# A fused GELU MLP, forward and backward: single steps up to pair 11 with x units as fill, and b2 added by VectorE

## The chip, the cores and the metric

The kernel runs on one core of a Trainium2 chip. The metric is the device time of one execution in microseconds (us). Engines: TensorE (PE, its weight loads PEld), VectorE (DVE), ScalarE (ACT), GpSimd (POOL) and SyncE (SP, which issues most transfers).

## The reference

An MLP with tanh-GELU, and all its gradients by `jax.vjp`; everything is bfloat16:

```python
B, S, D, F = 1, 2048, 448, 1792
h = gelu(x @ w1 + b1, approximate=True)      # (S, F)
out = h @ w2 + b2                            # (S, D)
# returns out and, for grad_out: grad x, grad w1, grad b1, grad w2, grad b2
```

So per block of rows the kernel needs u = x w1 + b1, h = gelu(u), out = h w2 + b2, q = grad_out w2^T, gh = q * gelu'(u), grad x = gh w1^T; at the end grad w1 = x^T gh and grad w2 = h^T grad_out, and the sums for the biases.

## The kernel before

**Tiling.** The 2048 rows are four blocks of 512 (0 to 3). F = 1792 is 14 tiles of 128, taken two at a time: a "pair" of tiles, seven per block, 28 in all. They are numbered k = 0 to 27 through the blocks; pair k belongs to block k // 7. For each one TensorE makes u (two banks of PSUM, [128, 512] each, list `PU`) and q (one double bank, `PQ`). D = 448 is three full tiles of 128 and a rest of 64 (`KF` = 3, `DL` = 64); the rest is the "tail" (`u_tail`, `q_tail`), a product over 64 rows of the array.

**Half products.** `half_product` (line 263) is a product over 64 of the 128 rows of the array, and `side_by_side` sends two of them, one on the lower and one on the upper half of the rows, into two different banks. A full product (lines 242, 303, 430) uses all 128 rows. Where halves and full products change places, a product of one kind follows one of the other.

**Units.** A "unit" is 128 rows of an output: kind "o" for out (from hT and w2), kind "x" for grad x (from ghT and w1T), with 14 tiles to be summed in one bank. Block by block there are four o units and four x units; `todo` holds them in that order, `open_unit` takes the next one and gives it a bank. They fill TensorE's time between the u and q products. `units_side` makes two units at once by halves: once with `second` False and once with True, so that each unit gets both halves of each tile. `pieces` and `Unit.emit` make them with full products. A unit that is finished waits in `finished` until `evictions` writes it out: by ScalarE (line 441) for x units and for the o units of block 0, whose b2 TensorE adds by a product with `row0`, a tile that has ones in two rows (`b2_of`); by VectorE with b2 added (line 443) for the other o units.

**The chain of a pair.** ScalarE or VectorE copies u out of its banks and adds b1 (`copy_u`, lines 346 and 348); ScalarE makes the square of u (line 355), gelu(u) into hT (352) and later a tanh (364). VectorE makes from the square the argument of the tanh ("cubic", "cubic*u"), from the tanh and h the slope of gelu ("slope", "slope*h", "both", "gate"), and at last `dve_gh` (line 400), gh = slope * q, which reads q's banks and frees them.

**Single steps and pairs.** The order on each engine is the order in which the code issues (`manual_schedule`); nothing reorders it. After the start (pairs 0, 1 and the u of 2) there are single steps i = 1 to 7 (`NSINGLE` = 8): a step makes u for f = i + 2 and q for i, with unit tiles between them (`between`). All these steps use banks 0 and 1 for u, and the double bank `two0` for q. From k = 8 on two pairs are taken at once (a loop over n, ks = [k, k + 1], fs = [k + 2, k + 3]), with instructions of double width; q's banks are then `two0` for even k and `two1` for odd k. In the first two of these rounds u, q and the units are full products (`pe_u_fulls`, `pe_q_fulls`, `pieces(28, ...)`); in the third only u is; after that everything is in halves, the u products of the round after next (`nxt`) are made ahead, and each round opens two units in `two1` as soon as gh has freed it.

In a single step ScalarE's order is tanh i, `evictions(2)`, copy f, `evictions()`, square f, gelu f. VectorE's order in the last single step, i = 7, is:

```python
dve_chain("both 7", "cubic*u 8", "gate 7", "cubic 9", "gh 7", "cubic*u 9")
```

The first two x units of block 0 are opened in `two1` at the end of step 6 and finished at the end of step 7; their eviction is issued at the head of the first pair round. In that round `dve_gate` and `act_tanh` stand at the head, so tanh of the two pairs needs "cubic*u" of both.

**Other lines.** `AZ` holds the squares and tanh arguments of three pairs in turn; `SETS`, `part_a` and `part_z` say where. `traffic` issues the transpositions of gh, the loads of the next block and, in step 6, `other_halves`; `stores` writes h to DRAM for the last phase. `g_low` is a copy of a tail of grad_out on the other half of the rows. After the blocks come grad w1 (line 742) and grad w2 (line 774) as full products.

Of the kernel before, what the change touches and what calls it, by code (L numbers as in the profile page):

```python
# [11 lines left out]
BF16 = mybir.dt.bfloat16  # L12
# [7 lines left out]
def kernel(  # L20
# [15 lines left out]
    nc = tc.nc  # L36
    P = 128
# [11 lines left out]
    NSTEP = NB * NPAIR  # L49
    NSINGLE = 8  # L50
    LEAD = 2
# [91 lines left out]
    nc.gpsimd.memset(b1_rows[:], 0.0)  # L143
    nc.vector.memset(row0[:], 0.0)
    for r0 in (0, DL):
        nc.vector.memset(row0[r0:r0 + 1, :], 1.0)
    nc.gpsimd.dma_start(out=b1_rows[0:NF, :], in_=b1.rearrange("(ft p) -> ft p", p=P))
# [48 lines left out]
    U4 = tmp.tile([P, 4, SB], BF16, name="U4", tag="U4", bufs=1)  # L196
    SETS = [8, 4]

# [121 lines left out]

    def unit_of(un, first, tiles):
        src, w = (hT, w2_sb) if un.kind == "o" else (ghT, w1T_sb)
        return lambda hf: [(un, un.ps, src[un.b][hf, t, un.j * P:(un.j + 1) * P], w[hf, 2 * FP[t // 2] + t % 2, :], hf,
                            first and t == 0, not first and t == NF - 1 and not un.b2_pe) for t in tiles]

    def b2_of(un):
        return lambda hf: [(un, un.ps, row0[hf, :], b2_bc[hf, :], hf, False, hf.start == (0 if un.j % 2 else DL))]

    def units_side(uns, second, tiles=range(NF)):
        one, other = uns[::-1] if second else uns  # L330
        side_by_side(unit_of(one, not second, tiles), unit_of(other, not second, tiles))
        if second and tiles[-1] == NF - 1:
            if one.b2_pe:
                side_by_side(b2_of(one), b2_of(other))
# [82 lines left out]
    class Unit:  # L417
        def __init__(self, kind, b, j):
            self.kind, self.b, self.j, self.done, self.ps = kind, b, j, 0, None
            self.b2_pe = kind == "o" and b == 0  # L420
            self.by_act = kind == "x" or self.b2_pe

# [4 lines left out]
        def emit(self, p):  # L427
            src, w = (hT, w2_sb) if self.kind == "o" else (ghT, w1T_sb)
            for a in range(2):
                nc.tensor.matmul(self.ps, lhsT=src[self.b][:, 2 * p + a, self.j * P:(self.j + 1) * P],  # L430
                                 rhs=w[:, 2 * FP[p] + a, :], start=(p == 0 and a == 0),
                                 stop=(p == NPAIR - 1 and a == 1 and not self.b2_pe), skip_group_check=True)
            if p == NPAIR - 1 and self.b2_pe:
                nc.tensor.matmul(self.ps, lhsT=row0[:], rhs=b2_bc[:], start=False, stop=True, skip_group_check=True)
            self.done += 1

        def evict(self):
            st = stg.tile([P, SB], BF16, name="st", tag="st")
            r = ROW0[self.b] + self.j * P
            if self.by_act:  # L440
                nc.scalar.copy(out=st[:, 0:D], in_=self.ps)  # L441
# [74 lines left out]
    uns = [open_units[0:2], open_units[2:4]]  # L516
    pieces(4, 0, -1)

# [3 lines left out]
    pe_tails([2], [0])  # L522
    side_by_side(q_of(0, 0), q_of(0, 1))
    units_side(uns[0], False, tiles(1))
    side_by_side(q_of(0, 1, True), q_of(0, 0, True))
    dve_chain("slope 0", "slope*h 0", "both 0", "cubic 1", "gate 0", "cubic*u 1", "slope 1", "gh 0", "slope*h 1")
    copy_u(2, "aa")
    act_tanh([1])
    act_square([2])
    act_gelu([2])  # L530
    for i in range(1, NSINGLE):
# [10 lines left out]
        units_side(*between[0])  # L542
        side_by_side(u_of(f, 1), u_of(f, 0))
        units_side(*between[1])
        pe_tail_pair(f, i, 1)
        pe_tail_pair(f, i, 0)
        units_side(*between[2])
        side_by_side(q_of(i, 0), q_of(i, 1))
        units_side(*between[3])
        side_by_side(q_of(i, 1, True), q_of(i, 0, True))  # L550
        if i < 6:
            units_side(uns[0], False, tiles(i + 1))
        if i > 1:
            act_tanh([i])
        evictions(2)
        copy_u(f, "aa")
        evictions()
        act_square([f])
        act_gelu([f])
        if i == 1:  # L560
            dve_chain("both 1", "cubic 2", "gate 1", "cubic*u 2", "slope 2", "gh 1", "slope*h 2", "cubic 3")
        elif i < 7:
            dve_chain(f"both {i}", f"cubic*u {i + 1}", f"gate {i}", f"slope {i + 1}", f"gh {i}", f"slope*h {i + 1}", f"cubic {f}")
        else:
            dve_chain("both 7", "cubic*u 8", "gate 7", "cubic 9", "gh 7", "cubic*u 9")
        if i == 6:
            open_two(1, 2)
            uns = [open_units[-2:]]
            units_side(uns[0], False, range(0, 6))
# [6 lines left out]
    g_swap = {}  # L576
    g_low = const.tile([P, SB], BF16, name="g_low")
    nq = NSTEP // 2 - NSINGLE // 2

    def two_units(banks):  # L580
        for n in banks:
            open_unit(one_bank(n, "ps")[:, 0:D])
        return open_units[-2:]

# [10 lines left out]
    for n in range(nq):  # L595
        i = NSINGLE + n
        k = NSINGLE + 2 * n
        ks = [k, k + 1]
        fs = [k + 2, k + 3] if k + 2 < NSTEP else []
        nxt = [k + 4, k + 5] if n >= 2 and k + 4 < NSTEP else []  # L600
        if n == 0:
            evictions()
        act_tanh(ks)
        dve_gate(ks, evictions)
        if n <= 2:
            for f in fs:
                pe_u_fulls(f)
        if n < 2:
            pe_tails(fs, ks)
            for q in ks:  # L610
                pe_q_fulls(q)
            for f in fs:
                copy_u(f, "aa")
            for q in ks:
                dve_gh(q)
            open_one()
            pieces(28, k + 1, k - 1)
            act_square(fs)
            act_gelu(fs)
            evictions(1)  # L620
            dve_cubic(fs)
        else:
            if fs:
                pe_tails(fs[::-1], ks[::-1])
            for f in fs[::-1]:
                copy_u(f, "aa")
            pe_q_rows(ks, nxt)
            for q in ks[::-1]:
                dve_gh(q)
            if nxt:  # L630
                open_u(nxt[0])
                side_by_side(u_of(nxt[0], 0, True), u_of(nxt[0], 1, True), slice(0, 1))
                open_two(1, 2)
                uns = open_units[-2:]
                units_side(uns, False)
                side_by_side(u_of(nxt[0], 0, True), u_of(nxt[0], 1, True), slice(1, None))
                units_side(uns, True)
                side_by_side(u_of(nxt[1], 1), u_of(nxt[1], 0))
                side_by_side(u_of(nxt[0], 1), u_of(nxt[0], 0))
            elif fs:  # L640
                uns, held = two_units(order_a[2:4]), two_units(order_a[0:2])
                units_side(uns, False)
                units_side(held, False)
                pe_tails([], [k + 2, k + 3])
                units_side(uns, True)
            if fs:
                act_square(fs)
                act_gelu(fs)
                dve_cubic(fs)
        if i == 8:  # L650
            nc.gpsimd.dma_start(out=g_low[0:DL, :], in_=gT[1][DL:P, 0, :])
            g_swap[1] = g_low
        if i == 15:
# [168 lines left out]
```

## Time and profile before

| | us |
|---|---|
| median of 3 runs | 269.21 (268.45 to 270.72) |
| profiled execution | 268.56 |
| its span | 266.8 |
| TensorE busy | 261.6 (98%) |
| VectorE busy | 173.4 (65%) |
| ScalarE busy | 138.7 (52%) |
| GpSimd busy | 40.3 (15%) |

The span runs from the first to the last instruction; the profiled execution's own time is longer by what lies around it. In lines of the timeline the columns are start, duration, engine, line of the code, operation, output and inputs, shapes, how many were merged, and in brackets the idle time ahead of it and what ended it. Ends of matmuls are modelled; the distance from one start to the next tells what one costs. In lines of waits: who waited for whom, us in total, times, longest.

### The profile page before, as it was taken

How to read it: one execution, taken by the hardware profiler on the slowest of the kernel's cores; microseconds unless marked ns; L12 is line 12 of the kernel's file. 1: busy time of each engine (PE TensorE's matmuls, PEld its weight loads, DVE VectorE, ACT ScalarE, POOL GpSimd, SP SyncE). 2: the span in 40 equal slices, each digit the busy share in tenths (PEclk: the TensorE clock that was granted, in tenths of full speed). 3: DMA queues.
4: the chain of work that ended last, by engine and by line, in shares of the span. 5: the costliest groups of instructions: out<-in, count | busy, mean ns of one | idle time of the engine just before them, and what ended most of it. 6: DMA issues, size and time to landing. Idle time of an engine off the chain costs nothing.

```text
span 266.8 us, 5001 instructions
## 1 busy us (share of the span) xinstructions
PE 261.6 (98%) x2082; PEld 159.9 (60%) x2082; DVE 173.4 (65%) x202; ACT 138.7 (52%) x162; POOL 40.3 (15%) x52
## 2 busy tenths in 40 slices
PE   7999999999999999999999999999999999999995
PEld 3367888744446565555658888864444765555554
DVE  2699997799998979669897731129999990000000
ACT  2899998899986686878659410022111111121111
POOL 1001004101002021010301020220700008900000
PEclk9999999999999999999999999999999999999999
DMA  7999999999999966264361359999511102999961
GB/s 160 252 227 211 175 213 188 288 232 206 259 225 257 220 172 170 54 164 94 111 157 43 72 120 256 357 197 230 138 39 39 52 20 58 200 225 225 161 163 34
DMA packets 111734, 44.46 MB, mean 167 GB/s; under 512 B 91040, under 2 KB 110576, under 8 KB 111712
## 3 DMA queue, kind: packets, MB, share of 16 engines
q1 hardware_dynamic: 104608, 36.14, 65.2%
q10 hardware_dynamic: 5248, 3.71, 5.6%
q0 software_dynamic: 1856, 4.30, 5.3%
q8 instruction: 16, 0.26, 0.4%
q14 instruction: 6, 0.05, 0.1%
HBM read 7.23 MB, written 14.23 MB: 80 GB/s over the span
## 4 chain that ended last, share of the span: by engine, by line
PE 94%; ACT 2%; DMA 2%; DVE 0%; issue 0%; ACTq 0%
PE ps L263 29%; PE ps_v L774 16%; PE ps_w L742 14%; PE pq L263 13%; PE pu L263 12%; PE pu L242 4%; PE ps_w L753 2%; PE pq L303 2%; PE ps L430 2%; DMA xT<-in_x_dram 2%; ACT AZ L355 1%; ACT hT L352 1%; DVE U L348 0%; ACT U L346 0%; ACT AZ L364 0%
## 5 line engine op out<-in xcount | busy, mean ns | idle before, releaser
L263 PE MATMUL ps<-w_sb,hT 64*128 64x448 bf16 x432 | 50.7, 349 | 0.3 <-ACT hT L352 0.3
L263 PE MATMUL pq<-gT,w2T 64*128 64x512 bf16 x338 | 49.9, 376 | 0.0
L774 PE MATMUL ps_v<-g_nat,h_nat 128*128 128x448 bf16 (+1 forms) x240 | 42.6, 340 | 0.0
L400 DVE SCALAR_TENSOR_TENSOR ghT<-AZ,pq 128x1024 bf16<-128x1024 bf16 x28 | 33.9, 1220 | 12.8 <-PE pq L263 11.8
L346 ACT ACTIVATE U<-pu,b1T 128x512 bf16<-128x512 f32 x54 | 33.3, 686 | 17.0 <-PE pu L263 12.7
L263 PE MATMUL ps<-w1T_sb,ghT 64*128 64x448 bf16 x392 | 40.8, 349 | 0.0
L444 POOL DMA_DIRECT2D out_dram<-st x32 | 18.9, 595 | 137.2 <-ACT st L441 84.0
L263 PEld LDWEIGHTS <-hT 64*128 64x128 bf16 x432 | 29.3, 94 | 13.7 <-ACT hT L352 0.8
L742 PE MATMUL ps_w<-gh_nat,x_nat 128*128 128x512 bf16 (+1 forms) x192 | 36.5, 352 | 0.0
L774 PEld LDWEIGHTS <-h_nat 128*128 128x128 bf16 x240 | 23.3, 98 | 19.3 <-DMA out_dram<-st 0.3
L263 PEld LDWEIGHTS <-ghT 64*128 64x128 bf16 x392 | 28.7, 94 | 9.2
L263 PE MATMUL pu<-xT,w_f 64*128 64x512 bf16 x228 | 33.1, 376 | 0.0
L263 PEld LDWEIGHTS <-w2T 64*128 64x128 bf16 x344 | 26.3, 94 | 9.5 <-PE pq L263 0.4
L364 ACT ACTIVATE AZ<-AZ 128x2048 bf16<-128x2048 bf16 (+1 forms) x18 | 27.5, 1526 | 7.4 <-DVE AZ L360 7.3
L728 DVE TENSOR_TENSOR acc<-acc,gh_nat 128x1792 f32<-128x1792 f32 x14 | 30.0, 2142 | 0.5
L742 PEld LDWEIGHTS <-x_nat 128*128 128x128 bf16 x192 | 18.7, 98 | 17.9 <-issue 0.4
L355 ACT ACTIVATE AZ<-U 128x1024 bf16<-128x1024 bf16 (+1 forms) x19 | 27.7, 1460 | 0.8 <-DVE U L348 0.4
L352 ACT ACTIVATE hT<-U 128x1024 bf16<-128x1024 bf16 (+1 forms) x20 | 27.6, 1383 | 0.0
L441 ACT CAST st<-ps 128x448 bf16<-128x448 f32 x20 | 9.8, 531 | 30.9 <-PE ps L263 28.7
L777 ACT CAST st<-ps_v 128x448 bf16<-128x448 f32 (+1 forms) x15 | 7.6, 507 | 34.8 <-PE ps_v L774 34.8
L745 ACT CAST st<-ps_w 128x512 bf16<-128x512 f32 (+1 forms) x12 | 6.4, 532 | 27.2 <-PE ps_w L742 27.2
L263 PEld LDWEIGHTS <-w_f 64*128 64x128 bf16 x228 | 15.6, 94 | 7.9 <-issue 0.2
(60 smaller groups left out, 214.2 us busy)
## 6 DMA issues: line engine op xcount, KB each, us to landing
hT_dram<-hT SPq DMA_DIRECT2D x28, 256.0 KB, 3.0
out_dram<-st POOLq DMA_DIRECT2D x32, 112.0 KB, 3.6
x_nat<-in_x_dram SPq DMA_DIRECT2D x1, 1792.0 KB, 10.7
g_nat<-in_grad_out_dram SPq DMA_DIRECT2D x1, 1792.0 KB, 16.3
out_dram<-st ACTq DMA_DIRECT2D x13, 112.0 KB, 3.6
out_dram<-st ACTq DMA_DIRECT2D x9, 128.0 KB, 1.9
w_f<-in_w_dram SPq DMA_DIRECT2D x5, 192.0 KB, 4.4
w_sb<-in_w_dram SPq DMA_DIRECT2D x4, 224.0 KB, 3.7
```

Source lines behind the costliest of these rows:

```text
L242: nc.tensor.matmul(PU[f][a][:, rs], lhsT=w1_f[:, kt, cols(p, a)], rhs=xT[b][:, kt, rs], start=(kt == 0 and rs.start == 0), stop=False, ski ...
L263: mm = nc.tensor.matmul(ps, lhsT=w, rhs=m, start=start, stop=stop, tile_position=(hf.start, 0), skip_group_check=True)
L346: nc.scalar.activation(out=dst, in_=PU[f][a][:], func=ACT.Identity, bias=bias)
L352: nc.scalar.activation(out=rows(hT, r), in_=part_u(r), func=ACT.Gelu_apprx_tanh)
L355: nc.scalar.activation(out=part_a(ks), in_=part_u(ks), func=ACT.Square, scale=math.sqrt(3.0 * GELU_A * GELU_C))
L364: nc.scalar.activation(out=z, in_=z, func=ACT.Tanh, scale=-1.0 / 3.0)
L400: nc.vector.scalar_tensor_tensor(out=rows(ghT, [k]), in0=part_z([k]), scalar=1.0, in1=PQ[k][:], op0=ALU.subtract if single else ALU.add, o ...
L441: nc.scalar.copy(out=st[:, 0:D], in_=self.ps)
L444: nc.gpsimd.dma_start(out=(out2 if self.kind == "o" else gx2)[r:r + P, :], in_=st[:, 0:D])
L728: nc.vector.tensor_tensor(out=v, in0=in0, in1=gh_nat[:, b, :, j, :], op=ALU.add)
L742: nc.tensor.matmul(ps[:, 0:n * P], lhsT=x_nat[:, st_, kt * P:(kt + 1) * P], rhs=gh_nat[:, b, ft0:ft0 + n, j, :], start=(st_ == 0), stop=(s ...
L774: nc.tensor.matmul(ps[:, 0:w], lhsT=h_nat[ft][:, st_, :], rhs=g_nat[:, st_, h * w:(h + 1) * w], start=(st_ == 0), stop=(st_ == NS - 1))
```

## The change

There are twelve single steps in place of eight (i up to 11), and the loop over pairs begins at k = 12, with all of its products in halves. Steps 7 to 11 each have ten pairs of unit halves as fill, taken from a list of 50: the rest of the first two x units (`ahead`, in `two1`), and the other two x units of block 0 (`later`, in banks 2 and 3). VectorE adds b2 to block 0's o units, as it does for all others; `row0`, `b2_of` and their products go. At the start only the first two units get a piece of full products ahead of the first tails; the first tiles of the other two (units Y and Z, `uns[1]`) come by halves after q's products. VectorE makes half of copy 2, "gate 0" moves behind "cubic*u 1". A unit is now finished by a count of its halves (`slots`).

```diff
-    NSINGLE = 8
+    NSINGLE = 12
-    row0 = const.tile([P, P], BF16, name="row0")
...
-    SETS = [8, 4]
+    SETS = [0, 8]
...
-        return place(4 * (k % 3) + 2 if k < NSINGLE else 2 * (k % 2), ks)
+        return place(4 * (k % 3) + 2 if k < NSINGLE else 4 + 2 * (k % 2), ks)
...
-    def b2_of(un):
-        return lambda hf: [(un, un.ps, row0[hf, :], b2_bc[hf, :], hf, False, hf.start == (0 if un.j % 2 else DL))]
...
-            if self.by_act:
+            if self.kind == "x":
                 nc.scalar.copy(out=st[:, 0:D], in_=self.ps)
...
     uns = [open_units[0:2], open_units[2:4]]
-    pieces(4, 0, -1)
+    for un in uns[0]:
+        un.emit(0)
...
     pe_tails([2], [0])
     side_by_side(q_of(0, 0), q_of(0, 1))
+    units_side(uns[1], False, tiles(0))
+    side_by_side(q_of(0, 1, True), q_of(0, 0, True))
+    units_side(uns[1], True, tiles(0))
     units_side(uns[0], False, tiles(1))
-    side_by_side(q_of(0, 1, True), q_of(0, 0, True))
-    dve_chain("slope 0", "slope*h 0", "both 0", "cubic 1", "gate 0", "cubic*u 1", "slope 1", "gh 0", "slope*h 1")
-    copy_u(2, "aa")
+    dve_chain("slope 0", "slope*h 0", "both 0", "cubic 1")
+    copy_u(2, "av")
+    dve_chain("cubic*u 1", "gate 0", "slope 1", "gh 0", "slope*h 1")
...
-            between = [(uns[0], False, range(6, 10)), (uns[0], False, range(10, 12)), (uns[0], False, range(12, 14)), (uns[0], True, range(0, 6))]
+            if i == 7:
+                ahead, later = xs, two_units((2, 3))
+                slots = [(ahead, False, t) for t in range(6, NF)] + [(later, False, t) for t in range(NF)]
+                slots += [(ahead, True, t) for t in range(NPAIR)] + [(later, True, t) for t in range(NF)]
+                slots += [(ahead, True, t) for t in range(NPAIR, NF)]
+            between = [slots[2 * c:2 * c + 2] for c in range(5)]
+            del slots[0:10]
...
         side_by_side(q_of(i, 1, True), q_of(i, 0, True))
         if i < 6:
             units_side(uns[0], False, tiles(i + 1))
+        elif i > 6:
+            fill(between[4])
         if i > 1:
             act_tanh([i])
-        evictions(2)
+        if i == 6:
+            evictions(2)
         copy_u(f, "aa")
-        evictions()
+        if i > 6:
+            evictions()
         act_square([f])
         act_gelu([f])
...
-            dve_chain("both 7", "cubic*u 8", "gate 7", "cubic 9", "gh 7", "cubic*u 9")
+            dve_chain(f"both {i}", f"cubic*u {i + 1}", f"gate {i}", f"cubic {f}", f"gh {i}", f"cubic*u {f}")
         if i == 6:
+            evictions()
             open_two(1, 2)
...
-        if i == 7:
-            units_side(uns[0], True, range(6, NF))
-        traffic(i)
+        if i == 9:
+            nc.gpsimd.dma_start(out=g_low[0:DL, :], in_=gT[1][DL:P, 0, :])
+            g_swap[1] = g_low
+        if i < 8 or i % 2:
+            traffic(i if i < 8 else (i + 7) // 2)
         if i >= 6:
-            stores(2, f - 1)
+            stores(1 if i > 7 and i % 2 else 2, f - 1)
...
+    def pe_u_rows(fs):
+        for f in fs:
+            open_u(f)
+            side_by_side(u_of(f, 0, True), u_of(f, 1, True))
+        for f in fs:
+            side_by_side(u_of(f, 1), u_of(f, 0))
...
     for n in range(nq):
-        i = NSINGLE + n
+        i = 10 + n
...
-        if n <= 2:
-            for f in fs:
-                pe_u_fulls(f)
-        if n < 2:
-            pe_tails(fs, ks)
...
+        if n == 0:
+            pe_u_rows(fs)
+        if fs:
+            pe_tails(fs if n == 0 else fs[::-1], ks[::-1])
```

In the new kernel's first pair round TensorE's order is: u of 14 and 15 (12 pairs of halves), their tails with those of q 13 and q 12, q 13, q 12, q 13, u 17, q 12, the first products of u 16, then two units in `two1`.

More of the change, by code (lines that the diff above doesn't have):

```diff
@@ L319, in q_of, with unit_of @@
                            for kt in range(1, KF + 1)]
-    def unit_of(un, first, tiles):
+    def unit_of(un, tiles):
         src, w = (hT, w2_sb) if un.kind == "o" else (ghT, w1T_sb)
         return lambda hf: [(un, un.ps, src[un.b][hf, t, un.j * P:(un.j + 1) * P], w[hf, 2 * FP[t // 2] + t % 2, :], hf,
-                            first and t == 0, not first and t == NF - 1 and not un.b2_pe) for t in tiles]
-    def b2_of(un):
-        return lambda hf: [(un, un.ps, row0[hf, :], b2_bc[hf, :], hf, False, hf.start == (0 if un.j % 2 else DL))]
+                            un.slots + n == 0, un.slots + n == 2 * NF - 1) for n, t in enumerate(tiles)]
     def units_side(uns, second, tiles=range(NF)):
         one, other = uns[::-1] if second else uns
[L331 to L334, printed above, removed]
+        side_by_side(unit_of(one, tiles), unit_of(other, tiles))
+        for un in uns:
+            un.slots += len(tiles)
+        if one.slots == 2 * NF:
             for un in uns:
@@ L431, in emit @@
                                  rhs=w[:, 2 * FP[p] + a, :], start=(p == 0 and a == 0),
-                                 stop=(p == NPAIR - 1 and a == 1 and not self.b2_pe), skip_group_check=True)
-            if p == NPAIR - 1 and self.b2_pe:
-                nc.tensor.matmul(self.ps, lhsT=row0[:], rhs=b2_bc[:], start=False, stop=True, skip_group_check=True)
+                                 stop=(p == NPAIR - 1 and a == 1), skip_group_check=True)
             self.done += 1
+            self.slots += 4
         def evict(self):
@@ L516, with two_units, fill @@
     uns = [open_units[0:2], open_units[2:4]]
-    pieces(4, 0, -1)
+    for un in uns[0]:
+        un.emit(0)
+    g_swap = {}
+    g_low = const.tile([P, SB], BF16, name="g_low")
+    def two_units(banks):
+        for n in banks:
+            open_unit(one_bank(n, "ps")[:, 0:D])
+        return open_units[-2:]
+    def fill(part):
+        if isinstance(part, tuple):
+            part = [(part[0], part[1], t) for t in part[2]]
+        for uns, second, t in part:
+            units_side(uns, second, [t])
     def tiles(p):
@@ L541 @@
         side_by_side(u_of(f, 0, True), u_of(f, 1, True))
-        units_side(*between[0])
+        fill(between[0])
         side_by_side(u_of(f, 1), u_of(f, 0))
-        units_side(*between[1])
+        fill(between[1])
         pe_tail_pair(f, i, 1)
         pe_tail_pair(f, i, 0)
-        units_side(*between[2])
+        fill(between[2])
         side_by_side(q_of(i, 0), q_of(i, 1))
-        units_side(*between[3])
+        fill(between[3])
         side_by_side(q_of(i, 1, True), q_of(i, 0, True))
@@ L599 @@
         fs = [k + 2, k + 3] if k + 2 < NSTEP else []
-        nxt = [k + 4, k + 5] if n >= 2 and k + 4 < NSTEP else []
+        nxt = [k + 4, k + 5] if k + 4 < NSTEP else []
         if n == 0:
@@ new lines @@
+        for f in fs[::-1]:
+            copy_u(f, "aa")
+        pe_q_rows(ks, nxt)
+        for q in ks[::-1]:
+            dve_gh(q)
+        if nxt:
+            open_u(nxt[0])
+            side_by_side(u_of(nxt[0], 0, True), u_of(nxt[0], 1, True), slice(0, 1))
+            open_two(1, 2)
+            uns = open_units[-2:]
+            units_side(uns, False)
+            side_by_side(u_of(nxt[0], 0, True), u_of(nxt[0], 1, True), slice(1, None))
+            units_side(uns, True)
+            side_by_side(u_of(nxt[1], 1), u_of(nxt[1], 0))
+            side_by_side(u_of(nxt[0], 1), u_of(nxt[0], 0))
+        elif fs:
+            uns, held = two_units(order_a[2:4]), two_units(order_a[0:2])
+            units_side(uns, False)
+            units_side(held, False)
+            pe_tails([], [k + 2, k + 3])
+            units_side(uns, True)
@@ L618 @@
+        if fs:
             act_square(fs)
             act_gelu(fs)
-            evictions(1)
             dve_cubic(fs)
[L622 to L649, printed above, removed]
```

30 lines of the change are left out of this document (4 added, 26 removed).

## Prediction

> **What bounds the kernel now.** I read the totals first, then TensorE's waits, then timelines around the places that the change touches. The totals and the waits:
>
> ```profile
> PE 261.6 (98%) x2082; PEld 159.9 (60%) x2082; DVE 173.4 (65%) x202; ACT 138.7 (52%) x162; POOL 40.3 (15%) x52
> PEclk9999999999999999999999999999999999999999
> PE pw L188 <- DVE AZ L142: 1.2, 1, 1.2
> PE pu L242 <- DMA xT<-in_x_dram: 0.4, 1, 0.4
> PE ps L263 <- ACT hT L352: 0.3, 1, 0.3
> ```
>
> TensorE is busy 98% of the span at full granted clock and waits for others three times, all before 15 us. So the time is TensorE's work plus whatever waits a change puts into it. VectorE's and ScalarE's work costs nothing until a TensorE instruction stands behind it.
>
> The second reading is what a product costs. TensorE around pair 12/13:
>
> ```profile
> 68.70 2.75 PE L242 MATMUL pu<-xT,w_f 128*128 128x512 bf16 x12
> 71.39 0.39 PE L263 MATMUL pu<-xT,wt 64*128 64x512 bf16 x1
> ...
> 72.26 2.11 PE L263 MATMUL pq<-gT,w2T 64*128 64x512 bf16 x18
> 74.21 0.81 PE L263 MATMUL pu<-xT,w_f 64*128 64x512 bf16 x6
> ...
> 75.72 2.81 PE L263 MATMUL ps<-w_sb,hT 64*128 64x448 bf16 x28
> ```
>
> Eighteen half products go from 72.26 to 74.21: 0.217 us for two side by side. Twelve full ones go from 68.70 to 71.39: 2.69, or 12 x 0.216 and 0.10 over. So two halves cost what one full product costs, and a change between the modes costs about 0.1. From 68.70 (first product for 14 and 15) to 75.72 (block 1's units open in `two1`) TensorE needs 7.02, 6.92 without the mode change.
>
> **Part 1, TensorE's own work.** 92 full products (36 of u, 24 of q, 28 and 4 of units) become 184 halves: nothing, by the rows above. The four b2 halves go:
>
> ```profile
> 38.86 0.46 PE L263 MATMUL ps<-b_bc,row 64*128 64x448 bf16 x2
> 39.05 0.91 PE L263 MATMUL pu<-xT,w_f 64*128 64x512 bf16 x6
> ```
>
> 39.05 - 38.86 = 0.19 twice, 0.38. Of the mode changes between step 7 and pair 12/13, five lie ahead of 68.70; four at 0.095 and the first at 0.2 (it also lets the slower half run out) make 0.58, and the sixth is the 0.10 already named. Bounds: 0.4 to 0.8 for all of them.
>
> The Trainium skill ("TensorE: Matmul & The Clock Gate", Part 3, The mechanism) says that a weight load overlaps a running product only where the row groups differ. By it the 92 full products would each show their load (98 ns at line 242), and the change would give 9.0 us. The equal spacing above speaks against it; it stands below as rival E.
>
> **Part 2, the start.** q for step 0 now follows 4 full unit products in place of 8, and the 0.43 between 13.69 and 14.12, spent waiting for gelu 1, is filled with units Y and Z, which need gelu 0 alone. TensorE would begin step 1 at 14.86, not 15.16. But VectorE also gets half of copy 2 ahead of "gate 0":
>
> ```profile
> 14.94 0.42 DVE L387 TENSOR_SCALAR AZ<-AZ 128x1024 bf16<-128x1024 bf16 x1
> 15.37 1.22 DVE L400 SCALAR_TENSOR_TENSOR ghT<-AZ,pq 128x1024 bf16<-128x1024 bf16 x1
> ```
>
> The copy costs 0.66 there (the spacing of the one at 10.81), so gh 0 ends at 17.25, not 16.59, and q's tail of step 1, which needs its bank `two0`, moves from 17.13 to 17.29. The gain is given back: +0.15. Bounds: -0.30 (if only the wait goes) to +0.5.
>
> **Part 3, b2 on VectorE.** In step 6 VectorE gets four evictions. A pair takes 1.16 at line 443, 1.07 until the next instruction starts. By the spacings of steps 4 and 5 gh 6 would start at 43.3 and end at 44.5, 0.6 later; the tail that needs it stands at 45.3. The second pair puts gh 7 at 48.7 to 49.9, against a tail at 50.25. Both are covered, the second by 0.3 only: 0, bounds 0 and 1.07. ScalarE loses four casts (1.9) in step 6, off the path. After that a step has ten unit pairs, so 14 x 0.216 + 10 x 0.189 = 4.91 of TensorE, while VectorE needs 4.31 (from gh 2 at 24.38 to gh 3 at 28.69 it has no idle time) and catches up by 0.6 a step.
>
> **Part 4, the end of the single steps: the wait that decides.** Every quantum of the five steps 7 to 11 is used up: the first x units (`ahead`, in `two1`) end with the last fill of step 11, immediately ahead of the u products for 14 and 15. Call that point T0. `evictions()` stands between copy 13 and square 13, so ScalarE's order is copy 13, two casts of `later`, two casts of `ahead`, square 13. The casts of `ahead` wait for T0, and square 13 is queued behind them. On VectorE "cubic 13" waits for square 13, and gh 11 and "cubic*u 13" are queued behind "cubic 13"; tanh of 12/13, the gate and gh 13 follow. In before the last step has gelu and square ahead of the casts:
>
> ```profile
> 42.02 0.97 ACT L441 CAST st<-ps 128x448 bf16<-128x448 f32 x2
> 42.88 1.07 ACT L355 ACTIVATE AZ<-U 128x1024 bf16<-128x1024 bf16 x1
> ...
> 47.87 1.06 ACT L355 ACTIVATE AZ<-U 128x1024 bf16<-128x1024 bf16 x1
> 48.83 1.04 ACT L352 ACTIVATE hT<-U 128x1024 bf16<-128x1024 bf16 x1
> 50.99 0.97 ACT L441 CAST st<-ps 128x448 bf16<-128x448 f32 x2 [1.12 <-PE ps L263]
> ```
>
> ```profile
> 48.96 0.43 DVE L383 TENSOR_SCALAR AZ<-AZ 128x1024 bf16<-128x1024 bf16 x1 [1.19 <-ACT AZ L355]
> 49.48 1.22 DVE L400 SCALAR_TENSOR_TENSOR ghT<-AZ,pq 128x1024 bf16<-128x1024 bf16 x1
> 50.62 0.68 DVE L385 TENSOR_TENSOR AZ<-AZ,U 128x1024 bf16<-128x1024 bf16 x1
> ...
> 54.60 1.23 DVE L375 TENSOR_TENSOR AZ<-AZ 128x2048 bf16<-128x2048 bf16 x1
> ```
>
> The chain from T0, each link from a row: the last products end 0.26 after T0 and the cast starts 0.04 later (50.95 to 50.99): 0.30. Two casts until the square: 42.88 - 42.02 = 0.86. Square to cubic: 48.96 - 47.87 = 1.09. Cubic to gh 11: 0.36. gh 11 to cubic*u 13: 50.62 - 49.48 = 1.14. From there over tanh to the end of the gate: 54.60 + 1.23 - 50.62 = 5.21. gh 13: 0.03 + 1.22, and 0.08 until `two1` is taken. Sum 10.29. TensorE has 6.92 of work there, so it stands still 10.29 - 6.92 = 3.37 between T0 and the opening of `two1`. It meets the lateness in pieces: q 12's tail waits for gh 11 (about 0.9), u 17's banks wait for copy 15, queued behind tanh 12/13 (about 1.3), `two1` waits for gh 13 (about 1.2). Later stages don't give it back, for TensorE has no other wait to shorten; VectorE regains its lead of some 1.1 in the next pair. Bounds 2.7 (ScalarE and VectorE overlapping more) to 4.1.
>
> **The sum.** T0 comes at 68.70 - 0.58 - 0.38 + 0.15 = 67.89, or 0.81 earlier. `two1` opens at 67.89 + 10.29 = 78.18 against 75.72: +2.46. Everything behind is the same program on TensorE. DMAs: the same transfers, gT of block 2 and g_low still one pair ahead of their use; two stores of h go ahead of a transposition in SP's queue (0.5 each to issue), hidden. The profiled execution took 268.56 (span 266.8); 268.56 + 2.46 = 271.0. The median of the runs is 269.21, 0.65 above it, so as a median 271.6.
>
> **Rivals.**
> - B, not slower: the chain of part 4 fits under TensorE's work, and only its savings show: -0.81 - 0.10 + 0.1 of waiting as before = -0.8, **268.4**. It decides if `two1` is free within 6.92 of T0. For it: at pair 14/15 VectorE is idle for 1.20 ahead of gh, at 85.87. Against it: ScalarE's order, which can't be passed.
> - C, VectorE falls behind after its four evictions: the 0.3 of cover at step 8 is missed and one pair (1.07) lands on TensorE as well: 271.6 + 1.1 = **272.7**. For it: VectorE is busy 19.3 of the 20 us from 20 to 40. Against it: the rows give 4.31 of work in 4.91.
> - D, the clock drops in the stall. The row of granted clock shows 9 in every slice, but the ten warm-up products start 0.43 apart, against 0.216 later, so a slow state exists. If it came back for as long as the warm-up, 4.3 us at half speed, +2.1: **273.7**. The Trainium skill (the same page, Part 1) puts the drop after an idle window of about 3.4 us. My pieces are near 1.3 each.
> - E, weight loads of full products are exposed now and the change hides them: 92 x 0.098 = 9.0, **260.2** with the b2 halves left aside.
>
> **How the numbers follow.** The forecast 0.63, B 0.15, C 0.13, D 0.05, E 0.04. The forecast's own range is 270.7 to 272.8. One per cent, about what a measurement can tell, is 2.7 us: to 271.9 the result counts as the same. Of the forecast 0.37 falls below that and 0.26 above; with B the same has 0.52, with C and D slower has 0.44, E is faster with 0.04. The range 268.2 to 273.2 holds B, C and the forecast's bounds and leaves out E and most of D.
>
> **What would show it.** Right: between T0 and `two1` TensorE has gaps behind gh 11, copy 15 and gh 13 of some 3.4 in sum; square 13 starts within 1.2 of the last x products; no b2 products; q's tail of step 1 near 17.3. Wrong: no gap of TensorE there, or gh 13 starting right at q 13's end; gaps in steps 7 to 8 (C); products 0.43 apart (D); pairs of halves closer than full products (E).

## The result and the profile after

| | before | after |
|---|---|---|
| median of 12 runs each, same chip | 268.54 us | 270.85 us |
| profiled execution | 268.56 | 270.53 |
| its span | 266.8 | 268.8 |

The ratio of the times is 1.0082, with a 95% interval of 1.0060 to 1.0104: the changed kernel is slower by 2.3 us, a little under one per cent. The forecast was 2.46 us slower. Here and below a ratio is that of the mean times without the slow runs (in before here the one of 272.82), so it differs a little from the quotient of the medians.

The totals and the row of granted clock of the page after:

```profile
PE 261.8 (97%) x2170; PEld 164.7 (61%) x2170; DVE 175.0 (65%) x214; ACT 137.3 (51%) x163; POOL 42.0 (16%) x52
PEclk9999999999999999999999999999999999999999
```

TensorE's busy time is what it was (261.8 against 261.6), the clock did not drop, and the span is 2.0 longer: all of it is TensorE standing still. Its waits (who waits for whom, us in total, times, longest):

```profile
PE pw L184 <- DVE AZ L141: 1.2, 1, 1.2
PE ps L259 <- DVE ghT L393: 1.1, 1, 1.1
PE pu L259 <- ACT U L339: 0.8, 2, 0.6
PE pq L259 <- DVE ghT L393: 0.4, 1, 0.4
PE pu L238 <- DMA xT<-in_x_dram: 0.2, 1, 0.2
```

The first and the last belong to the start and were there before; before's third, 0.3 for gelu 1, is gone. The three between are new, and they are the three of part 4: a unit in `two1` behind gh 13, u 17 behind copy 15, which frees its banks (L339 is the copy), q 12's tail behind gh 11 (L393). Where they fall is seen in TensorE's timeline from T0 on:

```profile
67.39 2.85 PE L259 MATMUL pu<-xT,w_f 64*128 64x512 bf16 x24
...
71.25 0.37 PE L259 MATMUL pq<-g_low,w2T 64*128 64x512 bf16 x1 [0.36 <-DVE ghT L393]
71.48 2.30 PE L259 MATMUL pq<-gT,w2T 64*128 64x512 bf16 x18
...
74.37 0.37 PE L259 MATMUL pu<-xT,w_f 64*128 64x512 bf16 x1 [0.59 <-ACT U L339]
74.94 0.80 PE L259 MATMUL pu<-xT,w_f 64*128 64x512 bf16 x5 [0.20 <-ACT U L339]
...
77.70 1.12 PE L259 MATMUL ps<-w_sb,hT 64*128 64x448 bf16 x10 [1.09 <-DVE ghT L393]
```

T0 is 67.39 and `two1` opens at 77.70: 10.31 us, where the profile of before has 7.02. The brackets add up to 2.24, which is less than the loss, because modelled ends of matmuls cover part of each wait. By the distances from one start to the next, less what the instruction ahead costs, the waits are 0.63 at q 12's tail, 1.2 at u 17 and 1.36 at `two1`, 3.2 in all. From there on nothing is lost or won: `two1` opens 1.98 later than before, and the profiled execution took 1.97 longer. (This execution began 0.38 earlier than before's: its first u product is at 5.38 and not at 5.76. Counted from there the two differ by 2.36.)

The cause, first on ScalarE:

```profile
66.31 0.96 ACT L431 CAST st<-ps 128x448 bf16<-128x448 f32 x2
67.68 0.97 ACT L431 CAST st<-ps 128x448 bf16<-128x448 f32 x2 [0.41 <-PE ps L259]
68.54 1.07 ACT L348 ACTIVATE AZ<-U 128x1024 bf16<-128x1024 bf16 x1
...
71.83 1.91 ACT L357 ACTIVATE AZ<-AZ 128x2048 bf16<-128x2048 bf16 x1 [1.28 <-DVE AZ L378]
```

The casts of `ahead` wait for TensorE's last x products (the 0.41 in brackets) and begin 0.29 after T0. Square 13 (L348), whose copy was made ahead of even the casts at 66.31, stands behind both pairs of casts until 68.54. Then VectorE:

```profile
65.73 0.69 DVE L387 TENSOR_TENSOR AZ<-AZ 128x1024 bf16<-128x1024 bf16 x1
69.64 0.43 DVE L376 TENSOR_SCALAR AZ<-AZ 128x1024 bf16<-128x1024 bf16 x1 [3.22 <-ACT AZ L348]
69.98 1.21 DVE L393 SCALAR_TENSOR_TENSOR ghT<-AZ,pq 128x1024 bf16<-128x1024 bf16 x1
71.11 0.68 DVE L378 TENSOR_TENSOR AZ<-AZ,U 128x1024 bf16<-128x1024 bf16 x1
75.10 1.22 DVE L368 TENSOR_TENSOR AZ<-AZ 128x2048 bf16<-128x2048 bf16 x1
76.42 2.35 DVE L393 SCALAR_TENSOR_TENSOR ghT<-AZ,pq 128x1024 bf16<-128x1024 bf16 x2
```

After gate 11 it is idle for 3.22, because "cubic 13" stands at the head of its queue and waits for square 13. gh 11 (69.98), queued behind it, needs nothing of pair 13; it runs only then, and q 12's tail waits for it. "cubic*u 13" at 71.11 starts tanh 12/13, which ends the gate at 76.32, and gh 13 follows.

### The profile page after: what moved, and what is told of

The parts are those of the page before. It is cut to its first block, busy times and chain, and to the rows that moved or that the text cites. A ratio compares the mean times of both kernels' runs of the same rounds, so it can differ in the third digit from the quotient of the medians.

```text
span 268.8 us, 5196 instructions
## 1 busy us (share of the span) xinstructions
PE 261.8 (97%) x2170; PEld 164.7 (61%) x2170; DVE 175.0 (65%) x214; ACT 137.3 (51%) x163; POOL 42.0 (16%) x52
## 4 chain that ended last, share of the span: by engine, by line
PE 94%; DMA 2%; ACT 1%; DVE 1%; issue 1%
PE ps L259 31%; PE ps_v L776 16%; PE pq L259 15%; PE pu L259 14%; PE ps_w L744 14%; PE ps_w L755 2%; DMA xT<-in_x_dram 2%; PE pu L238 2%; DVE ghT L393 1%; ACT U L339 0%; ACT st L431 0%; ACT AZ L348 0%; PE ps L421 0%; DVE AZ L378 0%; ACT st L779 0%
## 5 line engine op out<-in xcount | busy, mean ns | idle before, releaser
L259 PE MATMUL pq<-gT,w2T 64*128 64x512 bf16 x386 | 58.0, 376 | 0.0
L259 PE MATMUL ps<-w_sb,hT 64*128 64x448 bf16 x440 | 52.6, 349 | 1.1 <-DVE ghT L393 1.1
L259 PE MATMUL ps<-w1T_sb,ghT 64*128 64x448 bf16 x448 | 51.2, 349 | 0.0
L259 PE MATMUL pu<-xT,w_f 64*128 64x512 bf16 x300 | 44.0, 376 | 0.8 <-ACT U L339 0.8
L339 ACT ACTIVATE U<-pu,b1T 128x512 bf16<-128x512 f32 x53 | 32.8, 684 | 19.4 <-PE pu L259 19.4
L393 DVE SCALAR_TENSOR_TENSOR ghT<-AZ,pq 128x1024 bf16<-128x1024 bf16 x28 | 33.9, 1219 | 13.3 <-PE pq L259 12.6
L434 POOL DMA_DIRECT2D out_dram<-st x32 | 19.7, 618 | 137.8 <-DVE st L433 75.6
L259 PEld LDWEIGHTS <-ghT 64*128 64x128 bf16 x448 | 33.9, 94 | 10.3
L259 PEld LDWEIGHTS <-w2T 64*128 64x128 bf16 x392 | 29.8, 94 | 11.8 <-DMA w2T<-in_w_dram 0.3
L357 ACT ACTIVATE AZ<-AZ 128x1024 bf16<-128x1024 bf16 (+1 forms) x20 | 27.8, 1390 | 9.0 <-DVE AZ L353 7.3
L348 ACT ACTIVATE AZ<-U 128x1024 bf16<-128x1024 bf16 (+1 forms) x21 | 28.2, 1341 | 0.9 <-DVE U L341 0.4
L259 PEld LDWEIGHTS <-w_f 64*128 64x128 bf16 x300 | 21.0, 94 | 11.2 <-issue 1.4
L431 ACT CAST st<-ps 128x448 bf16<-128x448 f32 x16 | 7.8, 536 | 29.6 <-PE ps L259 28.0
```

The costliest lines, as they stand in the source:

```text
L259: mm = nc.tensor.matmul(ps, lhsT=w, rhs=m, start=start, stop=stop, tile_position=(hf.start, 0), skip_group_check=True)
L339: nc.scalar.activation(out=dst, in_=PU[f][a][:], func=ACT.Identity, bias=bias)
L348: nc.scalar.activation(out=part_a(ks), in_=part_u(ks), func=ACT.Square, scale=math.sqrt(3.0 * GELU_A * GELU_C))
L357: nc.scalar.activation(out=z, in_=z, func=ACT.Tanh, scale=-1.0 / 3.0)
L393: nc.vector.scalar_tensor_tensor(out=rows(ghT, [k]), in0=part_z([k]), scalar=1.0, in1=PQ[k][:], op0=ALU.subtract if single else ALU.add, o ...
```

## The experiments

Each kernel was run on one chip together with before, and each ratio is against before. The numbers that were compared in the traces are T0 and the opening of `two1`. The distance between them hardly depends on what happened earlier in that execution: after, e4 and e7 have the same program in this stage, their T0 lie at 67.39, 68.26 and 69.26, and the distances are 10.31, 10.36 and 10.36.

| kernel | median, before beside it | ratio (95%) | T0 | `two1` | between |
|---|---|---|---|---|---|
| after | 270.85, 268.54 | 1.0082 (1.0060 to 1.0104) | 67.39 | 77.70 | 10.31 |
| e1, casts of `ahead` later | 269.86, 268.86 | 1.0042 (1.0019 to 1.0065) | 68.77 | 77.71 | 8.94 |
| e2b, gh 11 first | 269.99, 268.86 | 1.0052 (1.0015 to 1.0090) | 68.17 | 77.52 | 9.35 |
| e2, both | 268.99, 268.86 | 1.0003 (0.9989 to 1.0017) | 68.29 | 76.39 | 8.10 |
| e6, no hold left | 268.09, 268.75 | 0.9980 (0.9964 to 0.9996) | 67.61 | 75.44 | 7.83 |
| e8, e6 with gT earlier | 268.16, 268.55 | 0.9975 (0.9958 to 0.9992) | 67.83 | 75.65 | 7.82 |

In e6 and e8 TensorE does 0.43 more work ahead of `two1` than in the others.

### e1: the casts of `ahead` behind square and gelu 13

```diff
         copy_u(f, "aa")
-        if i > 6:
-            evictions()
+        if i == NSINGLE - 1:
+            evictions(2)
         act_square([f])
         act_gelu([f])
+        if i > 6:
+            evictions()
```

Only the casts of `later` stay ahead of square 13, and these need nothing from T0.

> The changed kernel, but in step 11 the casts of the first x units (ahead) are issued behind square 13 and gelu 13; only the two casts of the other units (later) stay ahead of the square. Theory (square 13 is held by the casts that wait for the last fill): with the changed kernel's rows square 13 starts at 67.2, not 68.5, cubic 13 at 68.3, gh 11 at 68.6, cubic*u 13 at 69.7, gh 13 at 75.0, two1 opens near 76.3, not 77.70: 1.4 us less than the changed kernel, 269.4. Rival (VectorE is too slow for twelve single steps and holds the pair whatever ScalarE does): no change, 270.8.

ScalarE of this kernel:

```profile
67.69 0.96 ACT L431 CAST st<-ps 128x448 bf16<-128x448 f32 x2
68.53 1.09 ACT L348 ACTIVATE AZ<-U 128x1024 bf16<-128x1024 bf16 x1
...
70.43 0.98 ACT L431 CAST st<-ps 128x448 bf16<-128x448 f32 x2
```

T0 is 68.77 in this execution, so square 13 now starts 0.24 ahead of T0, where it started 1.15 behind it: 1.39 earlier. The distance to `two1` falls from 10.31 to 8.94, by 1.37. The link is shown: what square 13 gains arrives at `two1` whole. The ratio falls by 0.0040, or 1.1 us. The wait at q 12's tail is gone and that at u 17 falls from 1.2 to 0.5; the 1.35 at `two1` itself stays.

### e2 and e2b: gh 11 ahead of "cubic 13"

```diff
-            dve_chain(f"both {i}", f"cubic*u {i + 1}", f"gate {i}", f"cubic {f}", f"gh {i}", f"cubic*u {f}")
+            dve_chain(f"both {i}", f"cubic*u {i + 1}", f"gate {i}", f"gh {i}", f"cubic {f}", f"cubic*u {f}")
```

e2 has this edit and that of e1; e2b has it alone.

> As e1, and gh 11 is issued ahead of cubic 13. Theory: gh 11 starts right after q 11 (67.3), so q 12's tail waits for nothing; cubic 13 at 68.45, gate done at 74.0, two1 opens near 75.35: 2.35 us less than the changed kernel, 268.5, level with before; about 1.0 of waiting is left, which is VectorE's own work from gh 11 to gh 13 (7.9 us against 6.9 of TensorE's). Rival: no change, 270.8.

> The changed kernel with gh 11 issued ahead of cubic 13 and nothing else changed: the square still waits for the casts. Theory: the wait of q 12's tail goes (0.63), and gh 11's 1.14 leaves the chain behind the square: two1 opens at 76.5, not 77.70, 1.2 us less than the changed kernel, 269.65. If only q 12's wait counted (rival: the pieces are separate waits that add up), 0.6 less.

VectorE of e2:

```profile
68.21 1.22 DVE L393 SCALAR_TENSOR_TENSOR ghT<-AZ,pq 128x1024 bf16<-128x1024 bf16 x1 [0.89 <-PE pq L259]
69.34 0.42 DVE L376 TENSOR_SCALAR AZ<-AZ 128x1024 bf16<-128x1024 bf16 x1
```

gh 11 now waits for q 11's products instead, ends at 69.43, and q 12's tail finds its bank free. In e2 the only wait left between T0 and `two1` is about 1.04 at `two1`; the distance is 8.10, and the time is that of before (1.0003). In e2b the wait at q 12's tail is gone too, and of the other two that at `two1` stays and that at u 17 falls to 0.95:

```profile
PE ps L259 <- DVE ghT L393: 1.1, 1, 1.1
PE pu L259 <- ACT U L339: 0.5, 2, 0.3
PE pq L259 <- DVE ghT L393: 0.2, 1, 0.2
```

The last line is not q 12's tail but q 1's, at the start (17.57); part 2 comes back to it.

e2b's distance is 9.35, or 0.96 less than after's. That is more than the 0.63 that q 12's tail had lost: with gh 11 out of its way, "cubic 13" is followed by "cubic*u 13" at once, and the chain to gh 13 is shorter as well. So the two places in the order, ScalarE's casts and VectorE's gh, share the loss, 1.4 for the first and 0.8 to 1.0 for the second, and together they are worth 2.21 of the 3.29 that the stage had grown.

### e3: before with its first pair rounds in halves

In the first two rounds of before, u and q become halves; the units stay full products.

```diff
             for f in fs:
-                pe_u_fulls(f)
+                open_u(f)
+                side_by_side(u_of(f, 0, True), u_of(f, 1, True))
+            for f in fs:
+                side_by_side(u_of(f, 1), u_of(f, 0))
...
             for q in ks:
-                pe_q_fulls(q)
+                side_by_side(q_of(q, 0), q_of(q, 1))
+            for q in ks:
+                side_by_side(q_of(q, 1, True), q_of(q, 0, True))
```

> The kernel before, with the u and q products of the first pair rounds made by halves side by side (36 full products of u, 24 of q), the units' 28 left full. Theory (two halves cost what a full product costs, a change of mode 0.1 to 0.2): six changes of mode become four, 0.2 us less than before, 268.3. Rival (a full product shows its weight load of 98 ns): 60 x 0.098 = 5.9 us less, 262.6.

It took 269.54 against 268.86, a ratio of 1.0015 (0.9985 to 1.0045). Rival E asks for 262.6 and is refuted. The 0.2 less that the theory expected did not show either: with the wait for gT at q 7's tail (0.79) taken out, the trace has 0.1 less than before up to T0, and 0.1 more from there to `two1` (7.13 for 7.02). TensorE of this kernel, where q's halves are followed by full products of units:

```profile
54.88 2.97 PE L263 MATMUL pq<-gT,w2T 64*128 64x512 bf16 x25
57.78 2.82 PE L430 MATMUL ps<-w1T_sb,ghT 128*128 128x448 bf16 x14
```

From 54.88 to 57.78 are 2.90: twelve pairs at 0.217 make 2.60, a single half 0.22, and 0.08 is left for the change to full products. The four such changes of these rounds stand 285 to 309 ns apart from the product ahead, where a product costs 0.216: 0.07 to 0.09 each. The Trainium skill ("TensorE: Matmul & The Clock Gate", Part 3, The mechanism) states in a list that a weight load overlaps a running product only where the row groups differ; ahead of that list it lets a load into the background weight buffer go ahead of running products as well. This trace differs from the list's "only": full products on all rows follow each other as fast as pairs of halves do, 0.216 against 0.217.

### e4: after with the start of before

`pieces(4, 0, -1)`, the order of q, units and VectorE's chain, and the copy of u 2 are those of before; the rest is after.

> The changed kernel with the start of the kernel before (eight full unit products ahead of the first tails, copy 2 by ScalarE alone, gate 0 ahead of cubic*u 1); the rest as changed. Theory (the new start gives back at q 1's tail what it wins at gelu 1): q's tail of step 1 stands where it stands in before, 0.15 earlier than with the new start; 270.7, between 270.35 and 271.15. Rival (the new start is a gain of its 0.3 to 0.4 of filled wait): 271.2. The difference may be too small to tell in the times; the trace decides by the place of q 1's tail.

It took 271.13 against 268.75, a ratio of 1.0096 (1.0062 to 1.0130), not to be told from after. q 1's tail starts 11.37 after the first u product, in after 11.44. Its stall is after's: distances of 740, 967, 577 and 1456 ns where after has 739, 965, 577 and 1463. In the times the start neither wins nor loses what these runs can show; the traces say more, under part 2 below.

### e5: before with b2 added by VectorE

```diff
-            self.b2_pe = kind == "o" and b == 0
+            self.b2_pe = False
```

> The kernel before with one part of the change alone: b2 added by VectorE in the eviction of block 0's o units, no products with row0. Theory: TensorE loses 2 x 0.19 and VectorE's four evictions in step 6 and 7 are covered there (gh 6 has 2.15 of slack, gh 7 2.88): 0.38 less than before, 268.15. Rival (VectorE is full in the single steps and each pair of evictions delays gh by 1.07): 1 us more, 269.6.

It took 268.89 against 268.75: 1.0005 (0.9971 to 1.0038). The 0.38 that was expected did not show in the times, though the interval does not exclude it either. The trace says where it would have gone. VectorE of this kernel:

```profile
39.90 1.15 DVE L443 TENSOR_TENSOR st<-ps,b_bc 128x448 bf16<-128x448 f32 x2
41.70 1.16 DVE L443 TENSOR_TENSOR st<-ps,b_bc 128x448 bf16<-128x448 f32 x2 [0.64 <-PE ps L263]
44.91 1.22 DVE L400 SCALAR_TENSOR_TENSOR ghT<-AZ,pq 128x1024 bf16<-128x1024 bf16 x1
```

In before's order both pairs of evictions stand ahead of step 6's chain, and the second waits for TensorE first. gh 6 ends at 46.12, some 0.3 after the place of q 7's tail. After's order, with the second pair behind the chain, is what makes the edit free. In this execution something else covers the 0.3:

```profile
45.70 0.38 PE L263 MATMUL pu<-xT,wt 64*128 64x512 bf16 x1
...
47.85 0.39 PE L263 MATMUL pq<-gT,w2T 64*128 64x512 bf16 x1 [1.77 <-DMA gT<-in_grad_out_dram]
```

q 7's tail waits for gT of block 1, the last of the start's loads in SP's queue. e8 to e10 come back to it.

### e7: after with block 0's evictions made twice

VectorE makes each of the four additions a second time, into a spare tile.

```diff
             else:
+                if self.b == 0:
+                    more = stg.tile([P, SB], BF16, name="more", tag="more", bufs=1)
+                    nc.vector.tensor_tensor(out=more[:, 0:D], in0=self.ps, in1=b2_bc[:], op=ALU.add)
                 nc.vector.tensor_tensor(out=st[:, 0:D], in0=self.ps, in1=b2_bc[:], op=ALU.add)
```

> The changed kernel with each of the four evictions of block 0's o units made twice by VectorE (the second copy of the sum goes to a tile that nothing reads). Theory (a pair of evictions costs VectorE 1.07, and the single steps have 1.03 of slack at step 7's tail and 0.67 at step 8's): gh 6 ends 1.07 later, a wait of about 0.1 at step 7's tail; gh 7 ends 2.14 later, a wait of 1.4 at step 8's; after that VectorE catches up. 1.5 us more than the changed kernel, 272.3. Rival (VectorE catches up without touching TensorE): 270.8.

It took 272.54 (four runs) against 268.75: 1.0135 (1.0096 to 1.0174), which is 1.4 us more than after by the ratios. In after, gh 6 and gh 7 are over in time:

```profile
42.73 1.22 DVE L393 SCALAR_TENSOR_TENSOR ghT<-AZ,pq 128x1024 bf16<-128x1024 bf16 x1
44.79 1.15 DVE L433 TENSOR_TENSOR st<-ps,b_bc 128x448 bf16<-128x448 f32 x2
48.00 1.22 DVE L393 SCALAR_TENSOR_TENSOR ghT<-AZ,pq 128x1024 bf16<-128x1024 bf16 x1
```

They end 1.03 and 0.67 ahead of the tails at 44.97 and 49.89. With the additions doubled gh 6 has 0.05 left, gh 7 is late and TensorE waits 0.89 for it, and 0.56 for the doubled evictions themselves (by distances from start to start; the lines show idle time, and 0.4 of the first is q 12's tail):

```profile
PE pq L259 <- DVE ghT L393: 1.0, 2, 0.6
PE ps L259 <- DVE st L436: 0.3, 1, 0.3
```

Rival C's mechanism exists, and the change stays 0.67 away from it. The two waits make 1.45, near the 1.5 that was expected, but they were expected both at q's tails, 0.1 and 1.4. That the evictions would hold the banks of the next x units had not been expected.

### e6: no hold left

e6 takes e2 and does more at once. The slopes of 12 and 13 are made singly in step 11, so that less stands between tanh 12/13 and gh 13. The first three pairs of halves of u 16 go ahead of the units in `two1`. q 14's tail goes ahead of q 15's in the next round, and two pairs of the other tile's u products move to between the two passes of the units. The main lines:

```diff
-            dve_chain(f"both {i}", f"cubic*u {i + 1}", f"gate {i}", f"cubic {f}", f"gh {i}", f"cubic*u {f}")
+            dve_chain(f"both {i}", f"cubic*u {i + 1}", f"open {i + 1}", f"slope*h {i + 1}", f"gate {i}", f"gh {i}", f"cubic {f}", f"cubic*u {f}",
+                      f"open {f}", f"slope*h {f}")
...
-            side_by_side(u_of(nxt[0], 0, True), u_of(nxt[0], 1, True), slice(0, 1))
+            side_by_side(u_of(nxt[0], 0, True), u_of(nxt[0], 1, True), slice(0, 1 if n else None))
             open_two(1, 2)
```

> e2, and three more edits that shorten what is left of the wait at pair 12/13: VectorE makes the slope of 12 and 13 singly, that of 12 in its idle time ahead of gh 11; TensorE makes all of u 16's first three pairs of products (0.43 more) ahead of the units in two1, and q 14's tail goes ahead of q 15's in the next round. Theory: from T0 the tanh of 12/13 ends 4.45 later as in e2, two1 can open at 7.84, TensorE has 7.35 of work: 0.5 of waiting where e2 has 1.1. 0.6 less than e2 and with it 0.6 less than before, 267.9. Rival (the time is set by VectorE's sum of work there, not by the chain): as e2, 268.5.

TensorE ahead of `two1`:

```profile
74.41 0.97 PE L259 MATMUL pu<-xT,w_f 64*128 64x512 bf16 x6
75.44 0.74 PE L259 MATMUL ps<-w_sb,hT 64*128 64x448 bf16 x6
```

From the six halves of u 16 to `two1` are 1.03, where three pairs cost 0.65: a wait of 0.3 to 0.4, and the stage has no other. The kernel is faster than before by 0.2%, 0.9980 (0.9964 to 0.9996), and than after. With the stall nearly gone, what parts 1 to 3 win is left over: from q 1's tail to T0 it takes 50.57, as after does, where before takes 51.57. Which of e6's edits took away the rest of the stall is not shown.

### e8, e9, e10: gT of block 1 a load earlier

```diff
-    for t0, t1 in ((0, 8), (8, NF)):
+    for t0, t1 in ((0, 8), (8, 12), (12, NF)):
+        if t0 == 12:
+            load_g(1)
         nc.sync.dma_start_transpose(out=w1T_sb[:, t0:t1, :], in_=w1[:, t0 * P:t1 * P])
-    load_g(1)
```

e8 is e6 with this, e9 is before with it. e10 is e9 with b2 on VectorE and the second pair of its evictions behind step 6's chain, as in after.

> e6, and the load of grad_out's block 1 (gT) is issued ahead of the last two of the fourteen tiles of w1T, not behind them. In seven profiles it landed between 42.4 and 47.8, and q's tail of step 7, which needs it, stands at 45.0 to 46.0. Theory (in some executions this load ends last and TensorE waits up to 2 us): gT lands some 1.1 earlier, the wait is not seen, the slow ones of the runs go; the median is 0 to 0.4 less than e6, 267.9, and the highest run under 269. Rival (the runs differ for another reason): median and spread as e6.

> The kernel before with the same move of the load and nothing else. Theory: in before the margin is 0.25 in its profile; fewer runs over 269.5 and a median 0 to 0.4 lower, 268.4. Rival: as before, 268.7, with the same spread.

> e9 with b2 added by VectorE, and the second pair of evictions of step 6 issued behind that step's chain, as the changed kernel has it (in e5 all four stood ahead of gh 6, which then ended 0.3 after the place of q's tail of step 7). Theory: no evictions on the path, the two pairs of b2 products gone: 0.38 less than e9. Rival (b2's products cost TensorE nothing): as e9.

e8 took 268.16 against 268.55, 0.9975 (0.9958 to 0.9992), the fastest by ratio, though e6's interval holds it; gT landed at 42.59 there and at 42.74 in e6's profiled execution, so that execution shows no gain for the move. e9 was slower than before and not 0 to 0.4 faster: 269.79 against 268.55, 1.0030 (1.0007 to 1.0052). In before the last tiles of w1T are needed at about 45.6, ahead of q 7's tail, so the load that was moved back is the one that TensorE then stands for. The wait in e9, whose profiled execution took 272.60, and in e10, whose loads are e9's:

```profile
PE ps L264 <- DMA w1T_sb<-in_w_dram: 2.2, 1, 2.2
```

```profile
PE ps L264 <- DMA w1T_sb<-in_w_dram: 1.3, 1, 1.3
```

e10 took 269.23 against 268.55, 1.0012 (0.9989 to 1.0034). That is 0.56 less than e9, where 0.38 was expected of the b2 halves; the two intervals overlap, so the times agree with the term and do not show it. The traces show it, under parts 1 to 3 below.

## Why the prediction was right

**The stage and the chain (part 4): right in place, order and size.** The distance from T0 to `two1` was forecast as 10.29 and was 10.31. Square 13 started 1.15 after T0 (0.30 + 0.86 = 1.16 forecast). The stall was forecast as 3.37, and the waits seen at the three places add up to 3.2. TensorE's work in the stage is a little more than the 6.92 assumed: e2 without its one wait takes 8.10 - 1.04 = 7.06, 0.10 of it because the 24 halves of u take 2.69 there (68.29 to 70.98), as the twelve full products did in before with their change of mode. 10.31 less 7.06 is 3.25. How the stall was dealt out was a little off: 0.63, 1.2 and 1.36 where 0.9, 1.3 and 1.2 stood. e1 and e2 show that the two queues named, ScalarE's casts and "cubic 13" ahead of gh 11, are its cause, and not just its company: moved away, they give back 2.21 of 3.29.

**T0 (parts 1 to 3): right.** From q 1's tail to T0 the forecast has 0.58 + 0.38 = 0.96 less than before. The profiles have 51.57 (17.13 to 68.70) before and 50.57 (16.82 to 67.39) after: 1.00 less. e3 shows mode changes of 0.07 to 0.09, a little under the 0.095 assumed. The b2 halves are seen in the step that has two of them: from the first tail of u in step 5 to that in step 6 TensorE takes 4.72 in before, e3 and e9, with the halves, and 4.54 in e5 and e10, without; that is the 0.19 of the forecast. Two such pairs leave 0.62 of the 1.00 for the changes of mode, where 0.58 stood. T0 itself came at 67.39 and not at 67.89. Of these 0.50 the earlier beginning of this execution is 0.38, which is luck.

**The start (part 2): the loss is there, the gain of 0.30 is not.** Counted from the first u product, gh 0 begins 0.56 later than in before (10.17 against 9.61), where 0.66 was forecast, and q 1's tail 0.07 later, where 0.15 stood. The start of one execution differs from that of another by more than this: after, e1, e2 and e2b are one program up to step 11, and their gh 0 begins at 15.55, 16.15, 16.46 and 16.30. But all thirteen traces together show the wait that was forecast. In six of the seven with the new start q 1's tail begins 0.05 after the end of gh 0 (0.23 in e8); in the six with the old start 0.45 to 0.55 after it. Counted from the first u product q 1's tail begins at 11.44 to 12.21 with the new start, in the middle 11.62, and at 11.37 to 11.51 with the old. The gain did not come: in after step 1 begins 9.35 after the first u product, in before 9.40. With four unit products fewer ahead of it q 0 meets its weights before they have landed. w2T lands at 11.80 in after and q 0's first tail starts at 11.84; in before it lands at 11.96 and the tail starts at 12.55. TensorE's weight loads in after:

```profile
11.84 0.09 PEld L259 LDWEIGHTS <-w2T 64*128 64x128 bf16 x1 [0.34 <-DMA w2T<-in_w_dram]
```

The prediction has no such wait. That its sum for the start is near is in part luck.

**VectorE's cover (part 3): right, and wider than worked out.** The second pair of evictions had 0.67 of cover, not 0.3. gh 6 and gh 7 came 0.2 to 0.4 earlier against their tails than the spacings of steps 4 and 5 gave (1.03 for 0.8, 0.67 for 0.3). e7 shows the cost once the cover is gone.

**The rivals.** B fell with the 10.31. C was 0.67 away. E is refuted by e3.

D, the clock that drops in the stall, did not happen in after: no slice shows a lower clock, with waits of 1.4 at most. But its mechanism is seen in e9's profiled execution. There TensorE stands still for w1T, 2.59 from one start to the next:

```profile
PEclk9999999799999999999999999999999999999999
48.08 0.55 PE L264 MATMUL ps<-w1T_sb,ghT 64*128 64x448 bf16 x4 [2.22 <-DMA w1T_sb<-in_w_dram]
...
49.88 1.52 PE L264 MATMUL pq<-gT,w2T 64*128 64x512 bf16 x6
51.16 1.76 PE L264 MATMUL ps<-w1T_sb,ghT 64*128 64x448 bf16 x12
```

Half a microsecond after it has started again the granted clock falls to 0.50, and it stays there until 52: the six halves from 49.88 to 51.16 take 1.28, where they cost 0.65 otherwise. The stalls of 1.64 in e10 and 2.15 in e5, counted in the same way from start to start, left the clock as it was, and so did after's longest, 1.46. D fell because the pieces stayed short, as the prediction had argued. One such execution does not say where between 2.15 and 2.59 the limit lies, or whether there is a fixed one. The Trainium skill ("TensorE: Matmul & The Clock Gate", Part 1), which the prediction cites, puts the drop after an idle window of about 3.4 us. This trace differs: the drop followed a shorter stall.

**The absolute time.** The forecast stood on 269.21, a median of three runs; twelve runs beside the changed kernel gave 268.54. Of the difference between 271.6 and 270.85 that anchor is 0.67 and the mechanism's size, 2.46 against 2.31, is 0.15; the sum, 271.67, had been rounded down by 0.07. What the prediction did not name is gT of block 1, below.

## What to carry to other kernels

Where a schedule is written out by hand, look in each engine's queue for an instruction that waits for the end of something and stands ahead of one that could already run: here two casts on ScalarE and one cheap "cubic" on VectorE made up most of a loss of 3.3 us on a third engine that had no slack. Work such a chain out link by link from start-to-start distances, compare it with what the bounding engine has to do in that stage, and the difference is the stall. Fill that is used up exactly at a change of phase leaves nothing to cover the wait that comes there; in e6, which among other things puts three pairs of later work there, 0.3 to 0.4 of 3.3 us was left.

## What the runs showed that was not expected

gT of block 1, the last load that SP issues at the start, landed anywhere from 42.4 to 47.8 us in the ten profiled executions that have it in its old place: 45.79 in before, 44.59 in after, 46.35 in e1, 47.80 in e5, 42.74 in e6. q 7's tail needs it at 44.97 in after and 46.04 in before, so some executions wait for it, by 0.5 in e1, e3 and e4 and 1.8 in e5, and others not at all:

```profile
PE pq L259 <- DMA gT<-in_grad_out_dram: 0.5, 1, 0.5
```

That line is e1's. A program that reaches this tail earlier, as after does (39.59 after its first u product, before 40.28), has less room for a late load; a profile of one execution cannot show how often that costs something. How much of the spread of the times comes from it stays open: e8 moved the load and its median is that of e6.
